# Reordering the first microseconds: tile 0's LayerNorm chain first, x1 on a second queue, the third tile through the DMA crossbar, later x in pairs

## Chip, cores, metric

One core of one Trainium2 chip. The metric is device time of one execution in microseconds (us), lower is better.

## The reference, cut to what matters

```python
x = A_x                                  # 1 x 2048 x 576, bf16
xn = _layernorm(x)
out = x + linear_attention(xn, wqkv, wo) + (gelu(xn @ w_gate) * (xn @ w_up)) @ w_down
# attention: q, k, v = xn @ wqkv; phi(t) = where(t > 0, t + 1, exp(t)); 32 heads of 18
```

The kernel works on 16 tiles of 128 rows. For each it needs LayerNorm, the transposed xn (`xnT`), K and Q, and the sum G = xn^T phi(K). TensorE's results go to PSUM, the memory called `ps_all` in the lines below, and the kernel copies the transposes out of it (L243). All this is the first 60 us of 517; the gated feed-forward network follows. The change touches the first 60 us only.

## The kernel before: the parts that matter

Loads at the start. SyncE (SP) and ScalarE (ACT) each issue DMAs on a queue of their own:

```python
load_x(0, 1)
load_w(1, nc.scalar)            # K: wqkv columns 576..1151, a 576 KB part, then a 72 KB part
nc.scalar.preload_act_table_set("natural_log_exp_and_others")
load_x(1, 1)
load_x(2, 2)
load_w(0)                       # Q
load_x(4, 4)
...
spin(NWARM)                     # L132: 38 matmuls of 128 columns into an unused bank
```

The order of instructions on each engine isn't written by hand. A list schedule inside the kernel makes it, from a rank of each step and from assumed times at which data land:

```python
X_AT = [3.30, 3.80, 5.60, 5.60] + [9.00] * 4        # landing of x tile 0, 1, 2, ...
W_AT = {1: 5.00, 0: 7.60}                           # landing of K's and Q's weights
for n in range(NS):
    for h in range(2):
        step(("stats", n, h), "DVE", 0.41, n - 2.2, after_x, ..., ready=x_at)     # L203
    step(("aggr", n), "DVE", 0.21, n - 2.1, ...)                                  # L206
    step(("rstd", n), "ACT", 0.49, n - 2.1, ...)                                  # L210, L211
    # n < 3: norm on VectorE (L224), transposes on TensorE (L239), copy out of PSUM (L243)
    # n >= 3: norm, then dma_start_transpose on SyncE (L246): the DMA crossbar transposes on the way
    # all: K and Q matmuls (L254), exp (L261), phi (L266), G (L285)
```

A step goes out when its engine is free and its inputs are assumed ready; among steps ready at once the lower rank wins. On the chip the order is then fixed. VectorE doesn't pass an instruction whose data is late: below, an aggregate whose inputs are ready at 4.39 us starts at 6.21, behind a statistic that waits for its data.

Of the kernel before, what the change touches and what calls it, by code (L numbers as in the profile page):

```python
# [8 lines left out]
ACT = mybir.ActivationFunctionType  # L9
# [6 lines left out]
P = 128  # L16
HP = 64
S = 2048
D = 576
# [3 lines left out]
NS = S // P  # L23
# [5 lines left out]
KT = 5  # L29
# [7 lines left out]
NWBUF = 4  # L37
WDS = 3
NWARM = 38
TD = 3  # L40
XW = 640
KLO = HP + 1
PKW = 578
# [14 lines left out]
def kernel(  # L58
# [11 lines left out]
    nc = tc.nc  # L70
# [4 lines left out]
    x_view = A_x.flatten_outer_dims().rearrange("(p n) d -> p n d", n=NS)  # L75
# [13 lines left out]

    x_sb = persist.tile([P, NS, D], BF16, name="x_sb")  # L90

    def load_x(n0, cnt):
        nc.sync.dma_start(x_sb[:, n0:n0 + cnt, :], x_view[:, n0:n0 + cnt, :])  # L93

    attn_cm = tc.tile_pool(name="attn", bufs=1)
    apool = attn_cm.__enter__()
# [8 lines left out]
    def load_w(which, on=nc.sync):  # L105
        c = slice(which * D, (which + 1) * D)
        on.dma_start(wqkv_sb[:, 0:4, c], A_wqkv[0:512, c].rearrange("(kt p) c -> p kt c", p=P))
        on.dma_start(wqkv_sb[0:HP, 4, c], A_wqkv[512:576, c])

    load_x(0, 1)  # L110
    load_w(1, nc.scalar)
    nc.scalar.preload_act_table_set("natural_log_exp_and_others")
    load_x(1, 1)
    load_x(2, 2)
    load_w(0)
    load_x(4, 4)
# [12 lines left out]
    def spin(count):  # L129

        for _ in range(count):
            nc.tensor.matmul(ps_all[:, 7, 0:P], lhsT=ident[:], rhs=ident[:], start=True, stop=True)  # L132
# [3 lines left out]
    xnT = persist.tile([P, KT, S], BF16, name="xnT")  # L136
# [58 lines left out]
    rstd = persist.tile([P, NS], F32, name="rstd")  # L195
# [4 lines left out]
    def ln_half(n, h):  # L200
        if h == 0:
            ln_raw[n] = asmall.tile([P, 2, nc.vector.BN_STATS_DIM], F32, name="stats")
        nc.vector.bn_stats(out=ln_raw[n][:, h, :], in_=x_sb[:, n, h * HALF:(h + 1) * HALF])  # L203

    def ln_aggr(n):
        nc.vector.bn_aggr(out=mv[:, n, :], in_=ln_raw[n][:])  # L206

    def ln_rstd(n):
        r = rstd[:, n:n + 1]
        nc.scalar.activation(out=r, in_=mv[:, n, 1:2], func=ACT.Ln, bias=eps_ln[:], scale=1.0)  # L210
        nc.scalar.activation(out=r, in_=r, func=ACT.Exp, scale=-0.5)  # L211

    def ln_bias(n):
        nc.gpsimd.tensor_scalar(
            out=nbias[:, n:n + 1], in0=mv[:, n, 0:1], scalar1=rstd[:, n:n + 1], scalar2=-1.0, op0=ALU.mult, op1=ALU.mult,
        )

    def ln_norm_act(n):
        nc.scalar.activation(
            out=xn[:, n, 0:D], in_=x_sb[:, n, :], func=ACT.Identity, bias=nbias[:, n:n + 1], scale=rstd[:, n:n + 1],  # L220
        )

    def ln_norm(n, c0=0, c1=D):
        nc.vector.tensor_scalar(  # L224
            out=xn[:, n, c0:c1], in0=x_sb[:, n, c0:c1], scalar1=mv[:, n, 0:1], scalar2=rstd[:, n:n + 1],
            op0=ALU.subtract, op1=ALU.mult,
        )

    vcopy, acopy = nc.vector.tensor_copy, nc.scalar.copy

    def tp_bank(b):
        return ps_all[:, b, :].bitcast(BF16).rearrange("p (k t) -> p k t", t=P)

    TP_BANK = (3, 1, 0)

    def transposes(n, k0=0, k1=KT, b=None):
        b = TP_BANK[n] if b is None else b
        for kt in range(k0, k1):
            nc.tensor.transpose(tp_bank(b)[:, kt, :], xn[:, n, kt * P:(kt + 1) * P], ident[:])  # L239

    def tp_copy(n, k0=0, k1=KT, b=None, copy=acopy):
        b = TP_BANK[n] if b is None else b
        copy(out=xnT[:, k0:k1, n * P:(n + 1) * P], in_=tp_bank(b)[:, k0:k1, :])  # L243

    def dma_transposes(n):
        nc.sync.dma_start_transpose(xnT[:, :, n * P:(n + 1) * P], xn[:, n, 0:640])  # L246
# [4 lines left out]
    def kq_mm(n, which, hf):  # L251
        c = which * D + hf * HALF
        for kt in range(KT):
            nc.tensor.matmul(  # L254
                ps_all[:, KQ_BANK[which] + hf, :HALF], lhsT=xnT[:, kt, n * P:(n + 1) * P],
                rhs=wqkv_sb[:, kt, c:c + HALF], start=(kt == 0), stop=(kt == KT - 1),
            )
# [142 lines left out]
    LAG = 0.08  # L400
# [6 lines left out]
    steps = {}  # L407

    def step(name, *args, **kw):
        steps[name] = _Step(*args, **kw)  # L410

    X_AT = [3.30, 3.80, 5.60, 5.60] + [9.00] * 4
    W_AT = {1: 5.00, 0: 7.60}

    for n0 in (8, 12):
        step(("x", n0), "SP", 0.50, n0 - 5.5, [], lambda n0=n0: load_x(n0, 4), ready=8.5, tail=3.0)
    for n in range(NS):
        after_x = [("x", n // 4 * 4)] if n >= 8 else []
        x_at = X_AT[n] if n < 8 else 0.0
        for h in range(2):  # L420
            step(("stats", n, h), "DVE", 0.41, n - 2.2, after_x, lambda n=n, h=h: ln_half(n, h), ready=x_at)
        step(("aggr", n), "DVE", 0.21, n - 2.1, [("stats", n, 0), ("stats", n, 1)], lambda n=n: ln_aggr(n))
        step(("rstd", n), "ACT", 0.49, n - 2.1, [("aggr", n)], lambda n=n: ln_rstd(n))
        if n == 0:
            for i, (k0, k1, b, eng) in enumerate([(0, 3, 3, "ACT"), (3, KT, 2, "DVE")]):
                step(("norm", n, i), "DVE", 0.25, n - 2.1 + i / 10, [("rstd", n)],
                     lambda k0=k0, k1=k1: ln_norm(0, k0 * P, min(k1 * P, D)))
                step(("tp", n, i), "PE", 0.20, n - 1.5, [("norm", n, i)], lambda k0=k0, k1=k1, b=b: transposes(0, k0, k1, b))
                step(("xnT", n, i), eng, 0.45, n - 2.1, [("tp", n, i)],
                     lambda k0=k0, k1=k1, b=b, eng=eng: tp_copy(0, k0, k1, b, acopy if eng == "ACT" else vcopy))  # L430
            ready = [("xnT", n, 0), ("xnT", n, 1)]
        elif n < TD:
            step(("norm", n), "DVE", 0.42, n - 2.1, [("rstd", n)], lambda n=n: ln_norm(n))
            step(("tp", n), "PE", 0.30, n - 0.9, [("norm", n)], lambda n=n: transposes(n))
            step(("xnT", n), "ACT", 0.69, n - 1.5, [("tp", n)], lambda n=n: tp_copy(n))
            ready = [("xnT", n)]
        else:
            if n % 2:
                step(("bias", n), "POOL", 0.15, n - 2.1, [("rstd", n)], lambda n=n: ln_bias(n))
                step(("norm", n), "ACT", 0.65, n - 2.1, [("bias", n)], lambda n=n: ln_norm_act(n))  # L440
            else:
                step(("norm", n), "DVE", 0.43, n - 2.1, [("rstd", n)], lambda n=n: ln_norm(n))
            step(("xnT", n), "SP", 2.10, n - 1.9, [("norm", n)], lambda n=n: dma_transposes(n), tail=0.6)
            ready = [("xnT", n)]
        for which, rank in ((1, n), (0, n + 0.6)):
            for h in range(2):
                r = rank + h / 100
                free = [("phi", n - 1, which, h)] if n else []
                step(("mm", n, which, h), "PE", 0.615, r, ready + free, lambda n=n, w=which, h=h: kq_mm(n, w, h),
                     ready=W_AT[which], tail=0.15)  # L450
                step(("exp", n, which, h), "ACT", 0.49, r + 0.10, [("mm", n, which, h)],
                     lambda n=n, w=which, h=h: kq_exp(n, w, h))
                step(("phi", n, which, h), "DVE", 0.44, r + 0.15, [("exp", n, which, h)],
                     lambda n=n, w=which, h=h: kq_phi(n, w, h))
        step(("G", n), "PE", 0.75, n + 1.15, [("phi", n, 1, 0), ("phi", n, 1, 1)], lambda n=n: g_accumulate(n, G_A))
    for i, (at, count) in enumerate([(5.80, 3), (6.20, 3)]):
        step(("spin", i), "PE", 0.1 * count, -1.0, [], lambda count=count: spin(count), ready=at)

    def in_order(steps):

        left, done, free, begun = dict(steps), {}, {}, []
        while left:
            able = []
            for name, s in left.items():
                if all(a in done for a in s.after):
                    at = max([s.ready, free.get(s.engine, 0.0)] + [done[a] + LAG for a in s.after])
                    able.append((at, s.rank, name))
            first = min(able)
            engine = left[first[2]].engine
            _, at, name = min((r, t, m) for t, r, m in able if left[m].engine == engine and t <= first[0] + 0.05)  # L470
            s = left.pop(name)
            free[engine] = at + s.took
            done[name] = at + s.took + s.tail
            begun.append((at, len(begun), name))
        return [name for _, _, name in sorted(begun)]
# [184 lines left out]
```

## Time and profile before

| | before |
|---|---|
| time, first 3 runs | 519.88 us median (519.77 to 520.21) |
| profiled execution | 518.57 us, span 516.6 |
| TensorE (PE) busy | 99% of the span, 97% of the chain |
| first K matmul | 8.35 us |
| K of tile 2 begins | 14.90 us |

The span is the time from the first to the last instruction, and times inside a trace count from its start. "K2" below means the ten matmuls that make K of tile 2, and so on.

### The profile page before, as it was taken

To read this page: it belongs to the slowest core of one execution; us is meant where nothing else is said; L and a number is where in the kernel's file an instruction comes from. 1 tells how busy PE (TensorE), PEld (TensorE's weight loads), DVE (VectorE), ACT (ScalarE), POOL (GpSimd) and SP (SyncE) were. 2 spreads that over 40 slices of the span, in tenths; PEclk is the share of its full clock that TensorE was granted. 3 is DMA by queue.
4 is the path that set the end of the run, shared out by engine and by line. 5 is a ranking of instruction groups with operands and counts; after the bars stand their busy time and mean duration, and the time that the engine had idled before them with its cause. 6 is when DMAs were issued, how large, how long until landed. Compare 5 with 4: busy or idle time off the path is not lost.

```text
span 516.6 us, 10582 instructions
## 1 busy us (share of the span) xinstructions
PE 509.7 (99%) x4496; PEld 309.7 (60%) x4496; DVE 202.6 (39%) x413; ACT 137.3 (27%) x267; POOL 8.3 (2%) x26
## 2 busy tenths in 40 slices
PE   7999999999999999999999999999999999999997
PEld 6888864444487744444677644444777544445775
DVE  6887447666601036766401133333101234333100
ACT  4987523223310023233100022332000133232000
POOL 3001000000000000000000000000000000000000
PEclk9999999999999999999999999999999999999999
DMA  8324718999910055667500155555100455540000
GB/s 287 61 59 107 197 32 217 286 291 268 235 34 13 13 144 143 179 164 166 149 11 19 55 154 159 158 144 156 34 13 13 126 158 142 160 117 1 13 11 24
DMA packets 117785, 60.86 MB, mean 118 GB/s; under 512 B 24810, under 2 KB 117162, under 8 KB 117738
## 3 DMA queue, kind: packets, MB, share of 16 engines
q1 hardware_dynamic: 117130, 59.52, 43.8%
q8 instruction: 35, 0.57, 0.5%
q10 hardware_dynamic: 608, 0.66, 0.4%
q14 instruction: 12, 0.10, 0.1%
HBM read 52.79 MB, written 2.36 MB: 107 GB/s over the span
## 4 chain that ended last, share of the span: by engine, by line
PE 97%; DMA 1%; ACT 0%; DVE 0%; issue 0%; SPq 0%
PE ps_all L309 54%; PE ps_all L607 27%; PE ps_all L254 8%; PE ps_all L285 4%; PE ps_all L612 4%; DMA x_sb<-in_A_x_dram 1%; PE ps_all L356 0%; ACT xnT L243 0%; PE ps_all L589 0%; PE ps_all L239 0%; DVE hT L579 0%; ACT gl L578 0%; DVE stats L203 0%; DVE res L615 0%; SPq L93 0%
## 5 line engine op out<-in xcount | busy, mean ns | idle before, releaser
L309 PE MATMUL ps_all<-xnT,wg 64*128 64x512 bf16 x1152 | 272.0, 376 | 0.0
L309 PE MATMUL ps_all<-xnT,wu 64*128 64x512 bf16 x1152 | 271.5, 376 | 0.0
L578 ACT ACTIVATE gl<-ps_all 128x512 f32<-128x512 f32 x144 | 86.0, 597 | 313.7 <-PE ps_all L309 313.7
L579 DVE TENSOR_TENSOR hT<-ps_all,gl 128x512 bf16<-128x512 f32 x144 | 99.2, 689 | 143.6 <-ACT gl L578 143.2
L309 PEld LDWEIGHTS <-wu 64*128 64x128 bf16 x1152 | 108.3, 94 | 68.2
L309 PEld LDWEIGHTS <-wg 64*128 64x128 bf16 x1152 | 108.3, 94 | 67.8
L607 PE MATMUL ps_all<-wd_sb,hT 128*128 128x288 bf16 x1152 | 147.1, 286 | 0.0
L607 PEld LDWEIGHTS <-hT 128*128 128x128 bf16 x1152 | 112.3, 98 | 30.0 <-issue 1.6
L615 DVE TENSOR_TENSOR res<-ps_all,x_sb 128x288 bf16<-128x288 f32 x32 | 14.6, 457 | 144.9 <-PE ps_all L612 144.9
L309 PE MATMUL ps_all<-xnT,wr 64*128 64x512 bf16 x288 | 54.7, 376 | 0.0
L254 PE MATMUL ps_all<-wqkv_sb,xnT 128*128 128x288 bf16 x320 | 42.2, 286 | 0.1
L254 PEld LDWEIGHTS <-xnT 128*128 128x128 bf16 x320 | 30.5, 98 | 7.3 <-ACT xnT L243 0.2
L261 ACT ACTIVATE phi_e<-ps_all,neg 128x288 f32<-128x288 f32 x64 | 30.1, 497 | 9.6 <-PE ps_all L254 6.9
L612 PE MATMUL ps_all<-m_sb,pqT 126*128 126x288 bf16 (+1 forms) x160 | 24.9, 286 | 0.0
L309 PEld LDWEIGHTS <-wr 64*128 64x128 bf16 x288 | 14.0, 94 | 17.3 <-issue 0.7
L285 PE MATMUL ps_all<-hT,xn 128*128 128x288 bf16 (+4 forms) x176 | 22.6, 275 | 0.2 <-ACT xnT L243 0.2
L285 PEld LDWEIGHTS <-xn 128*128 128x128 bf16 (+1 forms) x176 | 17.6, 101 | 4.3 <-issue 0.4
L612 PEld LDWEIGHTS <-pqT 126*128 126x128 bf16 (+1 forms) x160 | 15.5, 97 | 4.1
L266 DVE SCALAR_TENSOR_TENSOR pq<-phi_e,ps_all 128x288 bf16<-128x288 f32 x32 | 14.3, 452 | 9.0 <-ACT phi_e L261 8.8
L266 DVE SCALAR_TENSOR_TENSOR hT<-phi_e,ps_all 128x288 bf16<-128x288 f32 x32 | 14.0, 450 | 2.5 <-ACT phi_e L261 2.2
L203 DVE BATCH_NORM_STATS2 stats<-x_sb 128x6 f32<-128x288 bf16 x32 | 13.4, 438 | 3.1 <-DMA x_sb<-in_A_x_dram 3.1
L388 DVE SCALAR_TENSOR_TENSOR pn<-pq,den_d 128x504 bf16<-128x504 bf16 (+1 forms) x32 | 13.1, 449 | 0.0
(52 smaller groups left out, 98.0 us busy)
## 6 DMA issues: line engine op xcount, KB each, us to landing
wg<-in_B_w_gate_dram SPq DMA_DIRECT2D x72, 256.0 KB, 2.9
wu<-in_B_w_up_dram SPq DMA_DIRECT2D x72, 256.0 KB, 3.6
wd_sb<-in_B_w_down_dram SPq DMA_DIRECT2D x12, 432.0 KB, 5.1
wr<-in_B_w_gate_dram SPq DMA_DIRECT2D x72, 32.0 KB, 2.7
wr<-in_B_w_up_dram SPq DMA_DIRECT2D x72, 32.0 KB, 3.1
out_dram<-res SPq DMA_DIRECT2D x15, 144.0 KB, 1.8
x_sb<-in_A_x_dram SPq DMA_DIRECT2D x3, 576.0 KB, 7.6
wqkv_sb<-in_A_wqkv_dram SPq DMA_DIRECT2D x2, 576.0 KB, 6.3
```

What stands on the lines that cost most here:

```text
L203: nc.vector.bn_stats(out=ln_raw[n][:, h, :], in_=x_sb[:, n, h * HALF:(h + 1) * HALF])
L254: nc.tensor.matmul(ps_all[:, KQ_BANK[which] + hf, :HALF], lhsT=xnT[:, kt, n * P:(n + 1) * P], rhs=wqkv_sb[:, kt, c:c + HALF], start=(kt == ...
L261: nc.scalar.activation(out=e[:], in_=ps_all[:, KQ_BANK[which] + hf, :HALF], func=ACT.Exp, bias=neg1[:], scale=1.0,)
L266: nc.vector.scalar_tensor_tensor(out=(pq, pk)[which][:, n, hf * HALF:(hf + 1) * HALF], in0=e_tiles[n, which, hf][:], scalar=1.0, in1=ps_al ...
L285: nc.tensor.matmul(ps_all[:m, b, col:col + w], lhsT=xn[:, n, j0:j0 + m], rhs=pk[:, n, d0:d0 + w], start=(n == 0 and col == 0), stop=(n == ...
L309: return nc.tensor.matmul(self.outs[i], lhsT=self.lhs(i, rows, kt), rhs=self.rhs(i, rows, kt), start=start, stop=stop, skip_group_check=True,)
L388: nc.vector.scalar_tensor_tensor(out=pn[:].rearrange("p (c t) -> p c t", t=P)[:, c0:c1, :nh * DH].rearrange("p c (h e) -> p c h e", e=DH), ...
L578: nc.scalar.activation(out=gl[:], in_=ps_all[:, b[0], :], func=ACT.Gelu_apprx_tanh)
L579: nc.vector.tensor_tensor(out=hT[:, GUB * k + i, :], in0=ps_all[:, b[1], :], in1=gl[:], op=ALU.mult)
L607: nc.tensor.matmul(acc, lhsT=hT[:, f, j * P:(j + 1) * P], rhs=wd_sb[:, f, hs], start=(f == 0), stop=False,)
L612: nc.tensor.matmul(acc, lhsT=pqT[:rows, c, ts_], rhs=m_sb[:rows, c, hs], start=False, stop=(c == NCH - 1),)
L615: nc.vector.tensor_tensor(out=res[:, hs], in0=acc, in1=x_sb[:, n, hs], op=ALU.add)
```

## The change

The intent: start the useful work on TensorE earlier, by letting tile 0's chain run first, by bringing x1 in beside x0, by taking the third tile's transposes and copy off TensorE and ScalarE, and by loading x8 to x15 when they are needed. The core of the diff, with cuts:

```diff
-TD = 3
+TD = 2
     load_x(0, 1)
+    load_x(1, 1, nc.scalar)
     load_w(1, nc.scalar)
     nc.scalar.preload_act_table_set("natural_log_exp_and_others")
-    load_x(1, 1)
     load_x(2, 2)
...
-    X_AT = [3.30, 3.80, 5.60, 5.60] + [9.00] * 4
-    W_AT = {1: 5.00, 0: 7.60}
+    X_AT = [3.50, 4.20, 6.50, 6.50] + [9.50] * 4
+    W_AT = {1: 5.50, 0: 7.60}
-    for n0 in (8, 12):
-        step(("x", n0), "SP", 0.50, n0 - 5.5, [], lambda n0=n0: load_x(n0, 4), ready=8.5, tail=3.0)
+    for n0 in range(8, NS, 2):
+        step(("x", n0), "SP", 0.50, n0 - 5.5, [], lambda n0=n0: load_x(n0, 2), ready=1.6 * n0 + 2.0, tail=3.0)
+        lead = {0: -9.0, 1: 0.5}.get(n, 0.0)      # added to the rank of a tile's LayerNorm steps
-    for i, (at, count) in enumerate([(5.80, 3), (6.20, 3)]):
-        step(("spin", i), "PE", 0.1 * count, -1.0, [], lambda count=count: spin(count), ready=at)
+    step(("spin",), "PE", 0.11, -1.0, [("tp", 0, 1)], lambda: spin(2))
-    at = max([s.ready, free.get(s.engine, 0.0)] + [done[a] + LAG for a in s.after])
+    at = max([s.ready, free.get(s.engine, 0.0)] + [done[a] + LAG * (steps[a].engine != s.engine) for a in s.after])
```

Two smaller parts are among the cuts or easily missed: tile 1's normalisation, transposes and copy are split in two, as tile 0's were, and the six filler matmuls behind tile 0's transposes become two.

More of the change, by code (lines that the diff above doesn't have):

```diff
@@ L90, with load_x @@
     x_sb = persist.tile([P, NS, D], BF16, name="x_sb")
-    def load_x(n0, cnt):
-        nc.sync.dma_start(x_sb[:, n0:n0 + cnt, :], x_view[:, n0:n0 + cnt, :])
+    def load_x(n0, cnt, on=nc.sync):
+        on.dma_start(x_sb[:, n0:n0 + cnt, :], x_view[:, n0:n0 + cnt, :])
     attn_cm = tc.tile_pool(name="attn", bufs=1)
@@ L232, in tp_bank @@
         return ps_all[:, b, :].bitcast(BF16).rearrange("p (k t) -> p k t", t=P)
-    TP_BANK = (3, 1, 0)
+    TP_BANK = (3, 1)
     def transposes(n, k0=0, k1=KT, b=None):
@@ L410, in step @@
         steps[name] = _Step(*args, **kw)
-    X_AT = [3.30, 3.80, 5.60, 5.60] + [9.00] * 4
-    W_AT = {1: 5.00, 0: 7.60}
-    for n0 in (8, 12):
-        step(("x", n0), "SP", 0.50, n0 - 5.5, [], lambda n0=n0: load_x(n0, 4), ready=8.5, tail=3.0)
+    X_AT = [3.50, 4.20, 6.50, 6.50] + [9.50] * 4
+    W_AT = {1: 5.50, 0: 7.60}
+    for n0 in range(8, NS, 2):
+        step(("x", n0), "SP", 0.50, n0 - 5.5, [], lambda n0=n0: load_x(n0, 2), ready=1.6 * n0 + 2.0, tail=3.0)
     for n in range(NS):
-        after_x = [("x", n // 4 * 4)] if n >= 8 else []
+        lead = {0: -9.0, 1: 0.5}.get(n, 0.0)
+        after_x = [("x", n // 2 * 2)] if n >= 8 else []
@@ L419 @@
         x_at = X_AT[n] if n < 8 else 0.0
         for h in range(2):
-            step(("stats", n, h), "DVE", 0.41, n - 2.2, after_x, lambda n=n, h=h: ln_half(n, h), ready=x_at)
-        step(("aggr", n), "DVE", 0.21, n - 2.1, [("stats", n, 0), ("stats", n, 1)], lambda n=n: ln_aggr(n))
-        step(("rstd", n), "ACT", 0.49, n - 2.1, [("aggr", n)], lambda n=n: ln_rstd(n))
-        if n == 0:
-            for i, (k0, k1, b, eng) in enumerate([(0, 3, 3, "ACT"), (3, KT, 2, "DVE")]):
-                step(("norm", n, i), "DVE", 0.25, n - 2.1 + i / 10, [("rstd", n)],
-                     lambda k0=k0, k1=k1: ln_norm(0, k0 * P, min(k1 * P, D)))
-                step(("tp", n, i), "PE", 0.20, n - 1.5, [("norm", n, i)], lambda k0=k0, k1=k1, b=b: transposes(0, k0, k1, b))
-                step(("xnT", n, i), eng, 0.45, n - 2.1, [("tp", n, i)],
-                     lambda k0=k0, k1=k1, b=b, eng=eng: tp_copy(0, k0, k1, b, acopy if eng == "ACT" else vcopy))
-            ready = [("xnT", n, 0), ("xnT", n, 1)]
-        elif n < TD:
-            step(("norm", n), "DVE", 0.42, n - 2.1, [("rstd", n)], lambda n=n: ln_norm(n))
-            step(("tp", n), "PE", 0.30, n - 0.9, [("norm", n)], lambda n=n: transposes(n))
-            step(("xnT", n), "ACT", 0.69, n - 1.5, [("tp", n)], lambda n=n: tp_copy(n))
-            ready = [("xnT", n)]
@@ new lines @@
+            step(("stats", n, h), "DVE", 0.41, n - 2.2 + lead, after_x, lambda n=n, h=h: ln_half(n, h), ready=x_at)
+        step(("aggr", n), "DVE", 0.21, n - 2.1 + lead, [("stats", n, 0), ("stats", n, 1)], lambda n=n: ln_aggr(n))
+        step(("rstd", n), "ACT", 0.49, n - 2.1 + lead, [("aggr", n)], lambda n=n: ln_rstd(n))
+        if n < TD:
+            for i, (k0, k1, eng) in enumerate([(0, 3, "ACT"), (3, KT, "DVE")]):
+                b = TP_BANK[n] - i
+                step(("norm", n, i), "DVE", 0.25, n - 2.1 + lead, [("rstd", n)],
+                     lambda n=n, k0=k0, k1=k1: ln_norm(n, k0 * P, min(k1 * P, D)))
+                step(("tp", n, i), "PE", 0.20, n - 1.5 + lead, [("norm", n, i)],
+                     lambda n=n, k0=k0, k1=k1, b=b: transposes(n, k0, k1, b))
+                step(("xnT", n, i), eng, 0.48 if eng == "ACT" else 0.30, n - 0.88 + lead, [("tp", n, i)],
+                     lambda n=n, k0=k0, k1=k1, b=b, eng=eng: tp_copy(n, k0, k1, b, acopy if eng == "ACT" else vcopy))
+            ready = [("xnT", n, 0), ("xnT", n, 1)]
```

## The prediction, as put on record before the change ran

> **What bounds the kernel now.** I read the busy shares and the chain that ended last on the page first, then the waits of TensorE (PE), then the chain and the timeline of the first 16 us, because the diff touches nothing later than tile 15 of the attention stage.
>
> ```profile
> PE 509.7 (99%) x4496; PEld 309.7 (60%) x4496; DVE 202.6 (39%) x413; ACT 137.3 (27%) x267; POOL 8.3 (2%) x26
> PE 97%; DMA 1%; ACT 0%; DVE 0%; issue 0%; SPq 0%
> ```
>
> PE is both busiest and 97% of the chain. All its waits in the whole execution are these four:
>
> ```profile
> PE ps_all L239 <- DVE xn L224: 1.8, 1, 1.8
> PE ps_all L132 <- POOL ident masks.py:199: 1.4, 1, 1.4
> PE ps_all L285 <- ACT xnT L243: 0.2, 1, 0.2
> PE ps_all L589 <- DVE hT L579: 0.2, 1, 0.2
> ```
>
> So after its first useful matmul PE loses about 0.4 us. What can be won is the time before that matmul (the 38 warm-up matmuls of L132 look busy but do no work) and whatever PE work the change deletes. The chain of the start, in order of time:
>
> ```profile
> 1.25 4.56 DMA x_sb<-in_A_x_dram
> 5.81 0.02 issue
> 5.83 0.46 DVE stats L203
> 6.29 0.12 DVE mv L206
> ...
> 8.35 1.40 PE ps_all L254 x10
> ```
>
> The transfer in it is issued at 1.25, the second on that queue: it is x of **tile 1**. The timeline shows why tile 1 is on tile 0's chain:
>
> ```profile
> 3.57 0.82 DVE L203 BATCH_NORM_STATS2 stats<-x_sb 128x6 f32<-128x288 bf16 x2 [1.61 <-DMA x_sb<-in_A_x_dram]
> 5.83 0.46 DVE L203 BATCH_NORM_STATS2 stats<-x_sb 128x6 f32<-128x288 bf16 x1 [1.44 <-DMA x_sb<-in_A_x_dram]
> 6.21 0.19 DVE L206 BATCH_NORM_AGGREGATE mv<-stats 128x2 f32<-128x12 f32 x1
> ```
>
> Tile 0's two statistics end at 4.39, but VectorE (DVE) keeps program order and next comes a statistic of tile 1, whose data lands at 5.81. Tile 0's aggregate, ready at 4.39, starts at 6.21. The kernel's own list schedule caused it: it assumed tile 1 at 3.80.
>
> The trace's records of completed transfers (last of the 16 engines) give the landings: x0 3.55; K's weights, 576 KB part 5.10, 72 KB part 6.02; x1 5.81; x2-3 6.62; Q's weights 8.49 and 8.72; x4-7 10.13; x8-11 11.65; x12-15 13.10. From 3 us on the packets move some 370 KB per us, so a landing goes with the bytes ahead of it.
>
> **What the Trainium skill says.** (1) "DMA: Bandwidth & Descriptors", section "Issuing engines are not separate DMA queues": transfers issued by different engines run on the same 16 engines and interleave; a second issuer saves only issue time. The trace agrees: one DMA issue holds a queue 0.40 to 0.57 us, and the rate does not rise with two queues. (2) Same page, "Queues, rings and completion order": each engine goes round-robin between queues, packet by packet. The trace does not look like that: x1, issued at 1.25 by SyncE, moved no packet before 4.25, when the 512 packets of K's large part, issued at 0.80 by ScalarE, were nearly through; x1 in turn landed before K's small part, issued at 1.30. Here transfers go in order of issue across both queues. I use the measured order. (3) "TensorE: Matmul & The Clock Gate", Part 1: matmuls start 107 ns apart while cold and 56 ns when warm, after about 3.4 us of activity in a free-running window. The trace agrees: the 38 warm-up matmuls start 107 ns apart, the transposes from 7.44 on 56 ns apart. (4) Same page, "PE-mode transpose": it needs a copy out of PSUM; here it took 0.69 us of ScalarE (ACT) a tile.
>
> **The change, part by part.**
>
> *Tile 0's chain first.* Its rank falls by 9, and a wait on one's own engine no longer costs a lag in the schedule, so the aggregate comes right after the two statistics. From aggregate to first K matmul the before took 8.35 - 6.21 = 2.14 us (aggregate 0.12, the two ACT steps 0.5, normalise 0.4, transpose 0.4, copy 0.5). With x0 at 3.55 to 3.65 (x1 now shares its start) the aggregate is at 4.35 to 4.45. Following the new ranks by hand, both statistics of tile 1 come between aggregate and normalise and cost about 0.1. K's first matmul could start at 6.55: 1.8 us earlier, **if K's weights are there**.
>
> *x1 on ScalarE's queue.* x1 now starts beside x0, about 4.2. But K's two parts move from second and fourth place back behind x1, and x2-3 and Q's large part move up on the other queue. Issue times, with 0.45 us on SyncE and 0.45 to 0.50 on ScalarE: x0 and x1 at 0.80; x2-3 and K large at 1.25; Q large at 1.73 and K small at 1.75; Q small 2.2. The fit landing = 3.5 + KB/368 goes through K small (936 KB, 6.02) and x4-7 (2448 KB, 10.13), within 0.35 us of the others. So:
> (A) SyncE wins both ties, as x1 did over K small by 0.05 us in the before: x0, x1, x2-3, K large, Q large, K small. K small is byte 1800 KB, landing 8.4.
> (B) K goes first: K small at 936 to 1224 KB, 6.0 to 6.8. The new table of the diff says 5.5 for K and 6.5 for x2-3, so its author thinks of this order.
> The fifth matmul of each K group needs K small.
>
> *PE from there to tile 2's K.* New PE order by hand: transposes of 0, K0, transposes of 1, Q0, G0, K1, Q1, K2. Durations from the timeline: 10 K or Q matmuls 122.5 ns apart = 1.23; transposes of a tile 5 x 56 ns = 0.28; G 0.74. In the before K2 starts at 14.90 (8.35 + 6.55).
> Under A: four K0 matmuls early, six from 8.4 on end at 9.14; + 0.33 transposes + 1.23 + 0.74 + 1.23 + 1.23 = 13.90, **1.0 us gained**.
> Under B: K0 from 6.55 ends at 7.8, transposes to 8.1; Q0 then waits for Q's weights, still byte 1800 to 1872 KB as before, 8.5 for its first matmul; Q0 ends at 9.75; + 0.74 + 1.23 + 1.23 = 12.95, **1.95 us gained**.
> So Q's weights eat most of what tile 0 wins, whatever K does: that is the cap.
>
> *Third tile by DMA crossbar.* PE loses five transposes, 0.28 us, and ACT a 0.69 us copy; the copy is also behind the gap of 12.60 to 12.93 in the before (the 0.2 us wait at L285 above). Both are already inside the sums, which have neither. It adds a 2.6 us transfer (median from issue to landing). Tile 2's normalise ends at about 9.5 under B and 10.7 under A, so its columns land at 12.2 and 13.3, some 0.6 us ahead of K2 in both.
>
> *x8-15 in four pairs later.* They landed at 11.65 and 13.10, long before their use (counting statistics in the timeline, tile 8's come at 21.84 us). Later they free the DMA engines from 10 to 13 us for tile 2's transposition. The schedule asks for the first pair from 14.8 us, so about 3 us remain before its use. A pair is 288 KB, 0.8 us, and may delay a transposition behind it by that; tiles from 4 on have 2 us of slack (tile 4 landed at 19.34 for a K at 21.35), tile 3 only 0.8. Gain and cost both near 0.
>
> After tile 3 PE is saturated in steps of 3.2 us, and every later stage is PE's too, so a start that is earlier by g ends earlier by g.
>
> **Rivals.** *The wait moves to K's weights (A):* for it speak the measured order of issue and the near ties; against it the author's table. Gain 1.0: 518.9. *K first, Q's weights cap it (B):* gain 1.95: 517.9. *Nothing comes through,* because transposition of tile 2 or 3 lands late and PE stops before K2 or K3: slack of 0.6 us is thin; 0.5 us left, 519.4. *Everything comes through,* the whole 1.8 at the start plus 0.6 of deleted transposes and gap: it needs Q's weights by 8.1, which the bytes speak against; 2.4 us, 517.5. *A cold PE:* the clock record turns full at 5.78 in the before; if the window falls later than 6.55, K0's first matmuls run at half rate, at most 1 us and rarely; I take 0.1. A regression needs K small after 9.5 us, against 1800 KB.
>
> **Range and chances.** A and B at about one half each: mean gain 1.5 us (0.5 x 1.0 + 0.5 x 1.95, rounded), so 519.88 - 1.5 = **518.4 us**. The ends: from 2.4 us gained (517.5) to 0.5 gained (519.4); the runs of one kernel spread by 0.4. 2% is 10.4 us, more than all time before the first K matmul that any part of this change reaches, so faster by over 2%: 0.01, within 2%: 0.98, slower: 0.01.
>
> **What would show each step.** Right: aggregate of tile 0 near 4.4 with no wait behind it, x1 landing by 4.4, no wait of over 1 us before the statistics of tile 1, ten transposes instead of 15, one crossbar transfer more, K2 between 12.9 and 13.9. A or B is told by K small's landing (8.4 or below 6.8) and by whether PE stops inside K0 or before Q0. Wrong: x0 landing after 4 us because x1 shares its start; a stop of PE before K2 or K3 on the crossbar; the time above 519.4; or PE's waits after 20 us differing from the before.

## The result

| | before | after |
|---|---|---|
| median of 6 runs | 519.81 (518.50 to 520.21) | 518.10 (517.11 to 518.30) |
| ratio | | 0.9966, 95% interval 0.9953 to 0.9980 |
| profiled execution | 518.57 | 518.27 |
| first K matmul | 8.35 | 6.73 |
| K2 begins | 14.90 (Q1 from 13.67, ten matmuls 122.5 ns apart) | 14.40 |

Ratios are the mean time of one kernel's fast runs over that of the other's of the same rounds, so not quite the ratio of the medians quoted beside them.

The interval of the ratio lies below 1, so the gain is clear of the noise, though far under 2%. The time lies inside the range, at 518.1 for 518.4. But the two profiled executions differ by 0.3 us where the medians differ by 1.7. A result that is right in the sum and not in the traces needs explaining.

First what went as the prediction said. The timeline of VectorE after (start, duration, engine, line, operation, tiles; in brackets the idle time before it and what ended it):

```profile
3.71 0.82 DVE L203 BATCH_NORM_STATS2 stats<-x_sb 128x6 f32<-128x288 bf16 x2 [1.75 <-DMA x_sb<-in_A_x_dram]
4.57 0.21 DVE L206 BATCH_NORM_AGGREGATE mv<-stats 128x2 f32<-128x12 f32 x1
4.69 0.77 DVE L203 BATCH_NORM_STATS2 stats<-x_sb 128x6 f32<-128x288 bf16 x2
...
5.38 0.62 DVE L224 TENSOR_SCALAR xn<-x_sb,mv,rstd 128x384 bf16<-128x384 bf16 x2
```

Tile 0's aggregate follows its statistics at once, 1.64 us earlier than before, and tile 1's statistics no longer wait. Then the waits of TensorE after (total, times, longest, in us):

```profile
PE ps_all L254 <- DMA xnT<-xn: 1.0, 1, 1.0
PE ps_all L239 <- DVE xn L224: 0.7, 1, 0.7
PE ps_all L254 <- DMA wqkv_sb<-in_A_wqkv_dram: 0.4, 1, 0.4
PE ps_all L254 <- ACT xnT L243: 0.3, 1, 0.3
```

(Two lines with waits that are as before are cut.) The wait ahead of the transposes (L239) has shrunk from 1.8 to 0.7 us; three new ones stand in K's line L254. The chain after shows when:

```profile
1.73 6.05 DMA wqkv_sb<-in_A_wqkv_dram
7.78 0.05 issue
7.83 0.92 PE ps_all L254 x6
...
10.24 4.11 DMA xnT<-xn
14.35 0.05 issue
14.40 1.40 PE ps_all L254 x10
```

K0 stops after four of ten matmuls until K's small part lands at 7.78. And TensorE, done with Q1 at 13.27, stops until tile 2's crossbar transfer lands at 14.35, 4.11 us after its issue instead of the usual 2.6. The landings (last of 16 engines, from the trace's completion records):

| | before | after | in kernel a_ksmall below |
|---|---|---|---|
| x0 / x1 | 3.55 / 5.81 | 3.69 / 3.87 | 3.61 / 3.77 |
| x2-3 | 6.62 | 4.70 | 4.69 |
| K large / small | 5.10 / 6.02 | 6.29 / 7.78 | 9.19 / 4.88 |
| Q large / small | 8.49 / 8.72 | 8.46 / 8.69 | 9.57 / 6.36 |
| tile 2 by crossbar, issue to landing | none | 10.24 to 14.35 | 13.21 to 17.82 |

So three questions: why do the traces differ by less than the times, why was the crossbar transfer late, and which part of the change matters?

### The profile page after: what moved, and what is told of

It is laid out like the page before. It is cut to its first block, busy times and chain, and to the rows that moved or that the text cites. A ratio compares the mean times of both kernels' runs of the same rounds, so it can differ in the third digit from the quotient of the medians.

```text
span 516.2 us, 10568 instructions
## 1 busy us (share of the span) xinstructions
PE 509.0 (99%) x4487; PEld 308.6 (60%) x4487; DVE 203.4 (39%) x415; ACT 136.9 (27%) x266; POOL 8.3 (2%) x26
## 3 DMA queue, kind: packets, MB, share of 16 engines
HBM read 52.79 MB, written 2.36 MB: 107 GB/s over the span
## 4 chain that ended last, share of the span: by engine, by line
PE 95%; DMA 3%; ACT 1%; DVE 0%; ACTq 0%; issue 0%; SPq 0%
PE ps_all L309 54%; PE ps_all L604 27%; PE ps_all L254 6%; PE ps_all L609 4%; PE ps_all L285 3%; DMA xnT<-xn 2%; DMA wqkv_sb<-in_A_wqkv_dram 1%; ACT phi_e L261 0%; PE ps_all L356 0%; PE ps_all L586 0%; ACT xn L219 0%; DVE hT L576 0%; ACT gl L575 0%; DVE res L612 0%; ACTq L107 0%
## 5 line engine op out<-in xcount | busy, mean ns | idle before, releaser
L254 PE MATMUL ps_all<-wqkv_sb,xnT 128*128 128x288 bf16 x320 | 42.5, 286 | 1.8 <-DMA xnT<-xn 1.0
L254 PEld LDWEIGHTS <-xnT 128*128 128x128 bf16 x320 | 30.3, 98 | 9.8 <-DMA xnT<-xn 1.7
```

Source lines behind the costliest of these rows:

```text
L254: nc.tensor.matmul(ps_all[:, KQ_BANK[which] + hf, :HALF], lhsT=xnT[:, kt, n * P:(n + 1) * P], rhs=wqkv_sb[:, kt, c:c + HALF], start=(kt == ...
```

## The experiments

Twelve kernels ran, in three jobs of four, each beside the kernel before on the same chip and timed in five rounds. Short names stand for them. All outputs are right.

### b_again: the kernel before, unchanged

> The kernel before, once more, as a null test and for a second profile. The first timing gave the before 518.5 to 520.2 in six runs while its profiled run took 518.57, so the profile of before may be an unusually quick execution. Theory 1 (TensorE clock phase): the clock turns full at another time in this profile than at 5.78 us, and later than 8.35 us in the slow executions. Theory 2 (instruction fetch): one of the 16 KB instruction fetches meets a crossbar transfer that something waits for. Expected: ratio 1.000 within 0.001; times between 518.4 and 520.3; the first K matmul again at 8.3 to 8.4 us.

Measured: 519.82 (518.36 to 520.91), ratio 1.0001. The profile now fell on a usual execution (519.45). The timeline of TensorE, first of the earlier profile of before, then of this one:

```profile
7.80 0.50 PE L132 MATMUL ps_all<-ident 128*128 128x128 bf16 x6
8.35 1.40 PE L254 MATMUL ps_all<-wqkv_sb,xnT 128*128 128x288 bf16 x10
```

```profile
7.90 0.85 PE L132 MATMUL ps_all<-ident 128*128 128x128 bf16 x6
8.54 2.19 PE L254 MATMUL ps_all<-wqkv_sb,xnT 128*128 128x288 bf16 x10
```

The same ten K matmuls take 2.19 us instead of 1.40, and the first five start 240 ns apart instead of 122.5: TensorE is at half clock. The trace's clock record turns full at 10.17 us here and at 5.78 in the first profile. The profile's granted clock reads 1.00 for every stretch in both, since the record only begins there; the durations of equal matmuls show the truth.

Over all jobs the kernel before ran 43 times. Ten executions lie between 518.28 and 518.67 (mean 518.48), 33 from 519.40 up (mean 519.92), none between. I call them the quick and the slow cluster. Where the granted clock of the whole execution (its mean share of the full clock) is on record, 15 of 28 slow ones have 0.996 or 0.997, and all nine quick ones have 1.000; the slow profile above shows that a slow one can also read 1.00, since its half clock lies before the record. The first expectation for the first K matmul (8.3 to 8.4) was missed: 8.54, the transposes being slow too. Theory 1 is favoured; no instruction fetch met a transfer that anything waited for in these first 20 us.

### b_warm: the kernel before with a longer warm-up

```diff
-NWARM = 38
+NWARM = 54
```

> The kernel before with 54 warm-up matmuls instead of 38 and nothing else, so that TensorE stays busy until tile 0's transposes. Theory (clock): most executions of the before lose about 1.2 us because the 2 us of idling between the warm-up and the transposes lets the clock stay or fall back to half rate (full only at 10.17 us in its second profile, 5.78 in its first; times in two clusters, 518.4 to 518.7 and 519.5 to 520.1). Then all executions fall in the quick cluster: median 518.4 to 518.8, ratio 0.9975 to 0.998, first K still at 8.3 us. Rival (the clusters come from something else): two clusters as before, ratio 1.000; or the longer warm-up delays the transposes, ratio over 1.0005.

Measured: 518.69 (518.55 to 519.84), ratio 0.9982 (0.9970 to 0.9995). Four of five runs (518.55 to 518.81) lie at the quick cluster, one in the slow.

```profile
1.42 5.75 PE L132 MATMUL ps_all<-ident 128*128 128x128 bf16 x54 [1.42 <-POOL ident masks.py:199]
7.48 0.53 PE L239 MATMUL ps_all<-ident,xn 128*128 128x128 bf16 x5 [0.32 <-DVE xn L224]
8.39 1.40 PE L254 MATMUL ps_all<-wqkv_sb,xnT 128*128 128x288 bf16 x10
```

Not one useful matmul starts earlier than in the quick profile of before, yet the median falls by 1.2 us: sixteen idle matmuls of warm-up win 0.9 us on average, of the 1.74 that the change wins. The clock was half or more of what the changed kernel won.

The edit lengthens the warm-up and closes the idle stretch behind it at once. That the stretch counts by itself shows in kernels with the same 38 matmuls: with 1.8 us of idling (before) 10 of 43 runs were quick, with 1.45 (b_rank) two of six, and with 0.1 to 0.7 (the changed kernel and b_lead) only one of 16 looks like a lost clock.

### a_cold: the changed kernel with a shorter warm-up

```diff
-            nc.tensor.matmul(ps_all[:, 7, 0:P], lhsT=ident[:], rhs=ident[:], start=True, stop=True)
+            nc.tensor.matmul(ps_all[:, 7, 0:w], lhsT=ident[:], rhs=ident[:, 0:w], start=True, stop=True)
-    spin(NWARM)
+    spin(NWARM, 72)
```

> The changed kernel with the same 38 warm-up matmuls, but 72 columns wide instead of 128: the same number of TensorE instructions, so the instruction fetch stays where it is, but the warm-up ends at about 3.8 us instead of 5.4 and TensorE then idles 2 us before tile 0's transposes, as it did in the kernel before. Theory (the change gains by closing that idle stretch, which keeps the clock): most executions lose the clock again, full only at 8 us or later or half for one more stretch of 3.4 us; median 518.8 to 519.4, about 1 us slower than the changed kernel. Rival (the clock plays no part in the change's gain): 517.9 to 518.1 as the changed kernel.

Measured: 518.80 (518.26 to 519.54), ratio 0.9993 (0.9976 to 1.0010). Three runs at 518.26 to 518.50, three at 519.09 to 519.54.

```profile
1.42 2.46 PE L132 MATMUL ps_all<-ident 128*128 128x72 bf16 x38 [1.42 <-POOL ident masks.py:199]
5.79 0.71 PE L239 MATMUL ps_all<-ident,xn 128*128 128x128 bf16 x5 [1.91 <-DVE xn L224]
...
6.86 2.50 PE L254 MATMUL ps_all<-wqkv_sb,xnT 128*128 128x288 bf16 x10
...
14.51 1.40 PE L254 MATMUL ps_all<-wqkv_sb,xnT 128*128 128x288 bf16 x10 [0.46 <-DVE mv L206]
```

With the idle stretch of 1.9 us back, the changed kernel loses 0.7 us of median against its own 518.10, timed in another job, and 0.85 of mean (518.84 for 517.99). K0 takes 2.50 us, at half clock (2.50 includes the stop for K's small part). The size is at the lower edge of what was expected. But this profile is the quickest of the six runs, 518.26, and its clock record turns full only at 9.02 us: it did not keep the clock. The loss was hidden. Tile 2's crossbar transfer landed at 14.47, so the stop before K2 shrank from 0.96 to 0.46 us (last line): Q1 ended 0.6 us later than in the changed kernel's profile (13.90 for 13.27), K2 began only 0.1 us later (14.51 for 14.40). So the stop on the crossbar can cover a lost clock in the changed kernel too, and what the three slower runs lost was not profiled. In this job five of eleven runs of before were quick, more than in the others, which is why its ratio is so near 1.

### a_again: the changed kernel, unchanged

> The changed kernel once more. In its profile tile 2's crossbar transfer took 4.11 us instead of 2.6 and TensorE stopped 1.0 us before tile 2's K; at that moment (11.90 us) a 16 KB instruction fetch was under way. If the fetch is the cause and regular, this profile shows the same stop (0.8 to 1.2 us, fetch at 11.7 to 12.1 us). If it was an accident of one execution, the transfer lands in 2.6 us here and there is no stop. Time 517.1 to 518.4, ratio 0.9966 within 0.001.

Measured: 517.88 (517.30 to 519.38), ratio 0.9969.

```profile
14.14 1.40 PE L254 MATMUL ps_all<-wqkv_sb,xnT 128*128 128x288 bf16 x10 [0.84 <-DMA xnT<-xn]
```

The stop before K2 is there again, 0.8 us; the transfer took 3.99 us (10.10 to 14.10), a fetch running from 11.09 to 12.61, earlier than expected. The clock record turned full at 6.83, 0.03 us before K0. Of the eleven runs of the changed kernel only one (519.38) looks like a lost clock; its granted clock was 0.996, and one stretch of 3.4 us at half rate is 3.4 x 0.5 / 517 = 0.003 of the span.

### a_wide: the same warm-up in fewer instructions

The page of before lists a queue that nothing in the kernel issues:

```profile
q8 instruction: 35, 0.57, 0.5%
```

These are 16 KB instruction fetches (35 packets, 0.57 MB), one packet each. In the two profiles of the changed kernel one ran at 11.90 to 12.84 and at 11.09 to 12.61, and 18 of the crossbar's 256-byte packets, which take 18 ns (median), stood for 1.3 to 1.6 us in the first of them. The period, some 15 us, is that of TensorE: 54 load and matmul instructions per 3.2 us are 256 in 15.2 us, and between the first four fetches of before lie 252, 256 and 248 of them. So fewer TensorE instructions in the warm-up should move the fetch (the new parameters of `spin` are cut):

```diff
-NWARM = 38
+NWARM = 26
+    wide = const.tile([P, 192], BF16, name="wide")
+    nc.vector.memset(wide[:], 1.0)
-            nc.tensor.matmul(ps_all[:, 7, 0:P], lhsT=ident[:], rhs=ident[:], start=True, stop=True)
+            nc.tensor.matmul(ps_all[:, 7, 0:w], lhsT=ident[:], rhs=rhs[:], start=True, stop=True)
-    spin(NWARM)
+    spin(NWARM, wide, 192)
```

> The changed kernel with 26 warm-up matmuls of 192 columns for 38 of 128: the same 4.1 us of warm-up in 24 fewer TensorE instructions, so that the instruction fetch that TensorE triggers comes about 1.5 us later, at 13 us or after. Theory (the fetch meets the crossbar transfer): tile 2's transfer lands within 2.7 us of its issue, no stop before tile 2's K, 0.5 to 1.0 us quicker than the changed kernel, 517.0 to 517.4. Rival (the first crossbar transfer is slow by itself): it takes 3.9 to 4.1 us again and the time stays at 517.9 to 518.1.

Measured: **516.92** (516.41 to 517.28), ratio 0.9944 (0.9930 to 0.9957). The fetch came at 13.69, the transfer took 2.49 us (10.07 to 12.56), and TensorE's timeline has no stop from K1 to K2:

```profile
10.65 3.84 PE L256 MATMUL ps_all<-wqkv_sb,xnT 128*128 128x288 bf16 x30
14.33 0.91 PE L287 MATMUL ps_all<-hT,xn 128*128 128x288 bf16 x7
```

Thirty matmuls (K1, Q1, K2) without a break; G1, which follows them, begins 1.05 to 1.3 us earlier than in the changed kernel (14.33 for 15.38 and 15.63). The rival falls. It shows that moving the fetch removes the delay, not how the two transfers get in each other's way.

The other traces agree. In the first 55 us of all 14 profiles, 17 crossbar transfers had a fetch that began 0.6 to 2.2 us after their issue, and they took 3.26 to 4.61 us. Another 17 met one earlier or later and took 2.48 to 3.02, one of them 4.43. Of 119 with no fetch beside them 117 took 2.36 to 2.89; the other two are tile 2's in a_wide_four (3.29, behind loads of x) and one in a_ksp (3.88, cause not found).

### a_td3: the third tile back on TensorE

```diff
-TD = 2
+TD = 3
-    TP_BANK = (3, 1)
+    TP_BANK = (3, 1, 0)
+        if n == 2:
+            # norm, five transposes, one ScalarE copy, as in the kernel before
-        step(("G", n), ..., [("phi", n, 1, 0), ("phi", n, 1, 1)], ...)
+        step(("G", n), ..., [("phi", n, 1, 0), ("phi", n, 1, 1)] + [("xnT", 2)] * (n == 0), ...)
```

(Tile 2's transposes use a PSUM bank of G, so the first G has to come after them.)

> The changed kernel with the third tile back on TensorE (five transposes and a ScalarE copy, ahead of the first G). Theory (crossbar wait costs more than the transposes saved): TensorE loses the 1.0 us stop and gets back 0.28 us of transposes and about 0.3 us of a wait for the copy, so 0.4 to 0.7 us quicker than the changed kernel, ratio to before about 0.995. Rival (the stop is only in the profile): 0.3 to 0.6 us slower than the changed kernel, ratio about 0.998.

Measured: 517.53 (517.13 to 517.60), ratio 0.9957: 0.35 us (against a_again of the same job) to 0.6 us (against the first timing) quicker than the changed kernel. So as it stands the crossbar step costs more than it saves, and only because of the fetch: with the fetch moved (a_wide, in another job on another chip) it is the better choice by 0.6 us. The wait that is left here is a smaller one, for tile 3:

```profile
17.07 1.40 PE L254 MATMUL ps_all<-wqkv_sb,xnT 128*128 128x288 bf16 x10 [0.18 <-DMA xnT<-xn]
```

### b_lead: only the order, with measured landings

The loads of the kernel before, untouched; the rank of tile 0 as in the change; and a table that tells the truth:

```diff
-    X_AT = [3.30, 3.80, 5.60, 5.60] + [9.00] * 4
-    W_AT = {1: 5.00, 0: 7.60}
+    X_AT = [3.55, 5.85, 6.65, 6.65] + [10.15] * 4
+    W_AT = {1: 6.05, 0: 8.50}
```

(also `lead` = -9 for tile 0, no lag on one's own engine, and G after tile 2's copy.)

> The kernel before with tile 0's chain truly first by the schedule alone: same rank rule as the change, and the landing table set to the measured landings (x1 at 5.85), with every transfer issued as before; third tile still on TensorE. K is then whole at 6.0 us, not 7.7. Theory (the order on VectorE is the cause, moving x1 is not needed): first K at 6.6 to 6.8 us with no stop in it, ended at 8.0; time at or below the change without crossbar for the third tile, 517.2 to 518.0, ratio 0.995 to 0.997. Rival (x1's move is needed): tile 1's chain, whose data come at 5.8, stops TensorE before tile 1's K and the time is 518.3 or more.

Measured: 517.35 (517.07 to 517.55), ratio 0.9952 (0.9940 to 0.9965).

```profile
6.82 1.40 PE L254 MATMUL ps_all<-wqkv_sb,xnT 128*128 128x288 bf16 x10
8.77 0.77 PE L254 MATMUL ps_all<-wqkv_sb,xnT 128*128 128x288 bf16 x5 [0.55 <-DMA wqkv_sb<-in_A_wqkv_dram]
```

K0 runs through without a stop, K being whole at 6.42; then Q0 waits for Q's large part (8.73), the cap that the prediction named. The time is that of a_td3, which has x1 moved, within 0.2 us. Moving x1 isn't needed; a schedule that knows when x1 lands does the same.

### b_rank: only the rank, with the old table

The same without the two table lines.

> The kernel before with the rank rule of the change alone: tile 0 first, no lag on one's own engine, but the old landing table (x1 at 3.80) and the old order of transfers. The order that it gives on VectorE has both statistics of tile 1 between tile 0's aggregate and its normalisation. Theory (rank alone can't free tile 0, because the table is wrong): the normalisation still waits for x1 at 5.8 us and starts at 6.6 to 6.7 us; first K at 7.9 to 8.1 us, 0.3 us earlier than before, and the clock is still lost in most executions: 519.0 to 519.8, ratio 0.998 to 1.000. Rival: the rank is what matters, time near the 517.4 of the version with measured landings.

Measured: 519.30 (518.08 to 519.68), ratio 0.9996 (0.9978 to 1.0014).

```profile
4.70 0.21 DVE L206 BATCH_NORM_AGGREGATE mv<-stats 128x2 f32<-128x12 f32 x1
5.95 0.82 DVE L203 BATCH_NORM_STATS2 stats<-x_sb 128x6 f32<-128x288 bf16 x2 [1.04 <-DMA x_sb<-in_A_x_dram]
6.68 0.60 DVE L224 TENSOR_SCALAR xn<-x_sb,mv,rstd 128x384 bf16<-128x384 bf16 x2
```

The aggregate is early, but the schedule, believing that x1 lands at 3.80, puts tile 1's statistics into the pause while ScalarE works, and the normalisation waits behind them. First K at 8.01, 0.34 us earlier than before, and the two quick runs (518.08 and 518.14) lie as much below the quick cluster of before. In the whole no gain of rank alone is shown: the interval includes 1.

### a_ksmall: the small part of each weight first

```diff
+        on.dma_start(wqkv_sb[0:HP, 4, c], A_wqkv[512:576, c])
         on.dma_start(wqkv_sb[:, 0:4, c], A_wqkv[0:512, c].rearrange("(kt p) c -> p kt c", p=P))
-        on.dma_start(wqkv_sb[0:HP, 4, c], A_wqkv[512:576, c])
```

> The changed kernel with every 72 KB part of a weight issued ahead of its 576 KB part. K's small part was the last of K to land (7.78 us, behind part of Q's large one) and TensorE stopped 0.44 us in the first K group for it. Theory: K is whole at 6.3 to 6.6 us, no stop in the first K group, first K ends 0.6 us earlier; but Q's weights still land at 8.5 to 8.7 us and the stop moves there, so 0.2 to 0.4 us are kept at most up to tile 2, and none of it if tile 2's crossbar transfer still lands at 14.35 us. Rival: K's large part simply lands later by as much and nothing changes.

Measured: 521.63 (521.18 to 521.80), ratio 1.0034: slower than both kernels, which neither theory expected.

```profile
9.23 2.34 PE L254 MATMUL ps_all<-wqkv_sb,xnT 128*128 128x288 bf16 x10 [2.75 <-DMA wqkv_sb<-in_A_wqkv_dram]
```

The large parts of K (ScalarE's queue, issued at 1.81) and Q (SyncE's, 2.32) were now under way together, their packets in turn (from 6.5 to 7.0 us, 55 of ScalarE's queue and 103 of SyncE's), and landed at 9.19 and 9.57, K 3 us later than in the changed kernel. TensorE stood for 2.75 us, and the clock record fell to half from 9.49 to 12.91: K0 took 2.34 us instead of 1.40 on top. So in these traces transfers of two queues that are under way together do interleave; my "order of issue" was read from one that was issued while the other was well ahead. K's small part in the changed kernel fits this too: it landed between my A and B, its packets lying among those of Q's large one from 5.5 to 7.0 us.

### a_ksp: K, Q, x2-3 in this order on one queue

Third tile on TensorE, x1 alone on ScalarE's queue, and on SyncE's x0, K, Q, x2-3, x4-7; the table set to 3.65, 4.20, 8.60, 10.20 and 5.90, 7.90.

> A version built from the findings: the changed kernel with the third tile on TensorE, x1 alone on ScalarE's queue, and on SyncE's queue x0, K, Q, x2-3, x4-7. By my order of issue K lands at 5.9 to 6.1 and Q at 7.7 to 8.0, so TensorE has no stop in the first K or Q; x2-3 come at 8.6, in time for tile 2 on TensorE. Expected 0.5 us below the change with the third tile on TensorE: 516.9 to 517.2, ratio 0.9945 to 0.995. Rival: the late x2-3 stop tile 2 or 3 (statistics of tile 2 only from 8.6), and the time is 517.5 or more.

Measured: 517.84 (517.55 to 518.49), ratio 0.9964: the rival. The weights landed as wanted (K 6.31, Q 8.36) and K0 ran through, but:

```profile
10.54 1.03 PE L254 MATMUL ps_all<-wqkv_sb,xnT 128*128 128x288 bf16 x7 [0.57 <-DVE xnT L243]
```

K1 stopped for tile 1's copy out of PSUM. That copy stood on VectorE, from 10.20, behind tile 2's statistics, which waited for x2-3 (8.88) and began at 8.90. It is the fault of the kernel before over again: an instruction whose data is late, put ahead of one that is needed.

### a_wide_four: a_wide with x8 to x15 early, in fours

The two x-load lines of the diff undone.

> The changed kernel with the wider warm-up (no fetch beside tile 2's crossbar transfer) and x8-15 in two loads of four tiles issued early, as in the kernel before. Theory (pairs matter only because they keep the DMA engines free for tile 2's transfer): the two loads move until about 12.6 us, tile 2's transfer, issued at 10.1, lands at 13.3 us or later instead of 12.5, and TensorE stops 0.2 to 0.8 us before tile 2's K; 517.1 to 517.7 against 516.9. Rival (gain and cost both near 0, as predicted): 516.9 within 0.2 and the transfer lands in 2.6 us.

Measured: 517.69 (517.43 to 518.20), ratio 0.9974; against 516.96 for "best" in the same job, 0.7 us slower. The last early load landed at 12.77, tile 2's transfer, issued at 10.03, at 13.32:

```profile
10.61 4.16 PE L256 MATMUL ps_all<-wqkv_sb,xnT 128*128 128x288 bf16 x30
...
17.14 1.03 PE L256 MATMUL ps_all<-wqkv_sb,xnT 128*128 128x288 bf16 x7 [0.40 <-DMA xnT<-xn]
```

K1, Q1 and K2 take 4.16 us where a_wide needs 3.84: 0.3 us for tile 2's transfer behind the early loads, as the theory said. The stop before K3 (second line) is also 0.3 us longer than a_wide's, but not through the loads: a fetch at 14.36 lies beside tile 3's transfer, which took 3.40 us (13.70 to 17.10). So the pairs are worth some 0.3 us by themselves, by one profile, and the rest of the 0.7 is where the fetch happened to fall.

### best: a_wide with tile 3 earlier

```diff
-        lead = {0: -9.0, 1: 0.5}.get(n, 0.0)
+        lead = {0: -9.0, 1: 0.5, 3: -0.4}.get(n, 0.0)     # also for tile 3's bias and norm
-        n - 0.88 + lead                                   # rank of a tile's copy out of PSUM
+        n - 0.88 - 0.5 * n + lead
```

(and the first G after tile 1's copy, which reads one of G's banks. A version without that had garbage in that bank in the simulator, and did not run; that is my account and not on record.)

> The changed kernel with the wider warm-up, and tile 3's statistics and tile 1's copy out of PSUM ranked earlier. With the wider warm-up alone TensorE stopped 0.36 us before tile 3's K (from 16.18 to 16.54). Expected: that stop goes, tile 3's transfer is issued 0.5 us earlier (13.2 us), 516.5 to 516.9, ratio 0.9935 to 0.9945. Rival: the earlier normalisation of tile 3 on ScalarE delays tile 1's exponentials and the time stays at 516.9 or grows.

Measured: 516.96 (516.45 to 517.32), ratio 0.9956. The stop before K3 is gone; Q2 and K3, between G1 and G2, are one stretch of work:

```profile
15.26 2.61 PE L256 MATMUL ps_all<-wqkv_sb,xnT 128*128 128x288 bf16 x20
```

but K's small part landed 0.12 us later than in a_wide's profile (7.73 for 7.61), and the sum is the same within the noise. No gain over a_wide can be claimed; both beat the changed kernel by about 1 us.

## Why the prediction was right in the number, and where it was not

**The bound, and the passing-through: right.** TensorE's steps of 3.2 us follow each other whatever the start, and a start earlier by g ends earlier by about g: a_again began G1 0.8 us before the first profile of before and its last G also 0.8 us before. In the first profile of the changed kernel 0.3 us got lost on the way: the 20 matmuls from 29.17 take 2.92 us instead of 2.61, and tile 7's crossbar transfer, which they need, landed at 30.65, 4.25 us after its issue, with a fetch at 28.33. The prediction had put the slack of such tiles at 2 us.

**Tile 0's chain: right.** First K at 6.73 for 6.55, x0 landing 0.1 us later than assumed. b_rank and b_lead show what the prediction had read from the trace: the false landing time was the cause.

**K's weights, A or B: neither.** K's small part came at 7.78, between 8.4 and 6.8, its packets mixed with those of Q's large part on the other queue. The failed step is "Here transfers go in order of issue across both queues". The sum up to Q1 was still good: TensorE was through with Q1 at 13.27, inside the 12.95 to 13.9 given for K2.

**The crossbar: wrong.** The step was "so its columns land at 12.2 and 13.3, some 0.6 us ahead of K2 in both". The transfer took 4.0 to 4.1 us for 2.6 and stopped TensorE by 0.8 to 1.0 us, half of what the start had won. The rival was named ("slack of 0.6 us is thin"), its cause, the fetch, was not. It could have been seen coming. In the profile of before a fetch stood at 12.76, where the change puts a crossbar transfer, and the transfer issued at 40.96, with a fetch from 42.90, took 4.46 us; the median of 2.6 hides it.

**The pairs: mis-sized.** "Gain and cost both near 0" should have been some 0.3 us of gain, given a crossbar transfer at 10 us: the early loads would have been in its way (a_wide_four, one profile).

**The cold clock: mis-sized, and it decides.** "I take 0.1" for the changed kernel, and nothing for the kernel before. The before pays 519.92 - 518.48 = 1.44 us in 33 of 43 executions, 1.1 us on average, if the slow cluster is the clock. The changed kernel idles 0.1 to 0.7 us (two profiles) where the before idles 1.8 and pays it in perhaps one of eleven. Against quick executions of before the changed kernel (mean 517.99 of eleven) gains 0.5 us, below the 1.0 of A; the clock adds 1.1 us; 1.6 in sum over all runs. The prediction, which had 1.5, got there with a start too large by about 1 us and a clock too small by about 1 us. That the two errors cancel is luck. Its sum also set gaps that were read from a quick execution (518.57) against a median of mostly slow ones (519.88). b_warm shows the clock's part by itself; a_cold brings the half clock back, and part of the time.

A smaller reading: the prediction has the transposes from 7.44 on 56 ns apart; the first five start 56 to 118 ns apart, and only those of later tiles 56 throughout.

What stays open: how much of each unprofiled execution is clock; I infer it from the clusters, the granted clock (0.996 or 0.997 in 15 of 28 slow ones, in none of nine quick ones) and the two interventions; only one slow execution was profiled. How often the changed kernel loses the clock isn't settled by its times either, since the stop before K2 can cover the loss, as in a_cold. Why the fetch holds up the crossbar's packets isn't shown either.

## What to carry to other kernels

Compare the profiled execution's time with the median before reading anything from it: here it was 1.3 us quicker, where the first three runs spread by 0.4, and it showed the unusual case. The idle stretch of 1.8 us between warm-up and first useful matmul cost twice here, once as waiting and once, as far as the clusters tell, in 33 of 43 executions as half clock afterwards; filling it is one changed constant. A static order per engine is as good as the landing times that it was made from, so set them from the trace, and check what else, instruction fetches included, is under way when a transfer is placed where TensorE will wait for its landing.

## What the Trainium skill lacked or had wrong

- "TensorE: Matmul & The Clock Gate": its closing table asks for no idle gaps over about 3 us, and Part 1 puts the ramp penalty below 1% of a typical kernel's span and not worth fitting. Here a gap of only 1.8 us behind 4.2 us of warm-up went with the slow cluster in 33 of 43 executions; closing it by a longer warm-up brought four of five runs to the quick one (median 518.69 for 519.91). The 1.44 us between the clusters are 0.3% of the span, so the size agrees with the page, but on average (1.1 us) they are the larger part of what this change won.
- "Runtime: NRT & Kernel Launch", section "Instruction fetch mechanics", says that crossing a 16 KiB boundary is mostly hidden. It lacks what the fetch does to other transfers: tile 2's crossbar transfer took 4.11 and 3.99 us with a fetch and 2.49 without, which was 1.0 us of the time (a_wide). Issuing such a transfer held SyncE for 1.65 to 2.22 us in the three traces in which a fetch lay beside the issue of tile 3's (a_wide, best, a_wide_four), and for 1.20 to 1.36 us for most other tiles in these traces.
- "DMA: Bandwidth & Descriptors" has the engines go round-robin between queues, which the prediction doubted. The interleaving is borne out where both queues have long transfers under way (K and Q at 9.19 and 9.57 in a_ksmall), though not in equal turns (55 packets to 103 from 6.5 to 7.0 us). I found nothing there on the other case seen here: x1, issued 0.45 us after K's large part on the other queue, moved its first packet 3 us later (4.32).
